# A Hyena-style block with a SwiGLU feed-forward: residuals added from PSUM by VectorE, the half-filled 14th down chunk padded to 128 rows, and a new order of all engines

## The chip, the cores and the metric

The kernel runs on one core of a Trainium2 chip. TensorE multiplies (PE in the profile), VectorE (DVE), ScalarE (ACT) and GpSimd (POOL) work on tiles in SBUF, only TensorE writes results to PSUM, and DMA queues move data; SyncE (SP) issues most DMAs, GpSimd some. Each engine runs its own list of instructions in order and waits on semaphores for the others. The metric is the device time in microseconds of one execution: before the change a median of 253.91 us of 3 runs (253.81 to 254.88).

## What is computed

The input has 2048 tokens of 640 channels. A layer norm of `q` gates a long causal convolution, and a SwiGLU feed-forward follows; both have a residual. `ln` is a layer norm without weights, `*conv*` a causal convolution over the whole sequence.

```
kv  = (causal 4-tap filter of k, per channel) * v
y   = kv *conv* ssm_k  +  kv * ssm_D          # reference: rfft, product, irfft
h   = q + ln(q) * y
out = h + (silu(ln(h) @ w_gate) * (ln(h) @ w_up)) @ w_down      # 640 -> 1728 -> 640
```

1728 hidden columns are 13 chunks of 128 and one chunk of 64.

## The kernel before

The sequence is cut into four blocks of 512 tokens (block 0 to 3). The convolution is done with small Fourier transforms as matrix products with tables of cosines and sines, block against block. The names of the tasks carry the block:

- `tp` the taps as matmuls, `ke` and `kv` their evacuation from PSUM and the product with v;
- `kt`, `kf`, `xf` the transposed filter and the forward transforms, `kte`, `kfe`, `xfe` their evacuations to SBUF, `kb`, `xb` the butterflies on VectorE;
- `p02` and so on the products of spectra (block of x, block of y) on VectorE, L783, `yb` the butterflies before the inverse transform (L561 or, for blocks 2 and 3, L651);
- `iv` the inverse transform on TensorE (L939, L944), followed by evacuation on ScalarE (L954), gate by VectorE (L961), mean and square sums on ScalarE (L860, L862), variance on VectorE (L855), the power -0.5 on GpSimd (L857), normalisation (L1001 or L995) and a transposing DMA by SyncE (`ht`, L450) into `hnT`;
- `fg`, `fu` gate and up products on TensorE (L1049) for 256 tokens at a time, `sg` the silu (L1057), `su`, `sv` the evacuation of up (L1062, L1066, L1068), `mu` their product on VectorE (L1070);
- `dn` the down product of 128 tokens by 640 columns (L1135; the last tile of block 3 in two parts, L1012), `rs` its residual.

**The 14th down chunk.** It has 64 rows of `w_down`, and a matmul of 64 rows occupies half of TensorE's array. With `PAIR = True` the kernel keeps the left 320 columns of that chunk in partitions 0 to 63 and the right 320 in partitions 64 to 127 (`WdC`, `WdD`). A copy `gd` (L1112 on VectorE, L1111 on ScalarE) puts the hidden values of that chunk into partitions 64 to 127 too, and the two matmuls of 64 rows run at the same time. Every other token tile starts with the pair instead of ending with it, so that two pairs can meet.

**The residual.** For the blocks in `RD = (0, 1, 2)` ScalarE or VectorE moves the down product plus the mean of q (q is kept centred) from PSUM to the single buffer `RB` (L1151, L1152), and GpSimd issues a DMA that adds `RB` to `xh` in SBUF (`ra`, L568). SyncE then issues the output DMA (`out`, L1164). For block 3 VectorE does both in one `scalar_tensor_tensor` that reads PSUM (L1156).

**What sets the order.** `PLAN` holds, for each engine, the order of all tasks as numbers, and for each PSUM tile one of four units of two banks. The code adds waits where the data, or the earlier user of a unit, asks for it. Which engine does an evacuation is settled by the list in which it stands. The numbers count the tasks, so removing tasks renumbers the lists.

Of the kernel before, what the change touches and what calls it, by code (L numbers as in the profile page):

```python
# [50 lines left out]
class _Graph:  # L51
# [131 lines left out]
    def emit(self, block):  # L183
# [84 lines left out]
    "act":  # L268
# [9 lines left out]
    "dve":  # L278
# [15 lines left out]
        "806 ",  # L294
    "units":
        "0113201022031012033321231021332312133313321010001232312221313201230311022320230103301222001112012120120312322323013103"
        "23101021312302023330210213103130021301200122003201320321302",
    "fills": {
        "wb0": ["zmem", 3],
        "k0t4.0": ["zmem", 1],  # L300
# [945 lines left out]
```

## Time and profile before

| what | value |
|---|---|
| median of 3 runs | 253.91 us (253.81 to 254.88) |
| the profiled execution's own time | 254.13 us |
| its span, first to last instruction | 252.2 us |
| PE, DVE, ACT, POOL busy | 96%, 78%, 73%, 23% |
| granted TensorE clock | 1.000 |
| the copies `gd` on VectorE and on ScalarE | 5 of 0.22 us, 3 of 0.41 us |
| the residual DMAs `xh<-RB` | 12 of 160 KB, median 2.9 us from issue to landing |

The profile is one execution. Times in it are microseconds from the first instruction. A row such as `L783 DVE TENSOR_TENSOR tt<-XH,C 128x2560 bf16` gives the line of the kernel, the engine, the operation, what it writes and reads, and the shape; `xN` is a count. A number in square brackets is idle time of the engine just before, with what ended it. VectorE's instructions overlap at their ends by some hundredths, so what one costs in a dense stretch is the distance from its start to the next start.

### The profile page before, as it was taken

What the parts mean: (1) busy time and instruction counts of PE and PEld (TensorE: products, weight loads), DVE (VectorE), ACT (ScalarE), POOL (GpSimd) and SP (SyncE); (2) the same over time, 40 slices, a digit from 0 to 9 for tenths busy, and PEclk for the clock granted to TensorE, in tenths of its full rate; (3) what the DMA queues carried; (4) which work ended last, traced back from release to release, by engine and by line L of the source; (5) the groups of instructions that cost most, each with busy time, mean ns of one, the idle gap of its engine ahead of it and who ended that gap; (6) DMA issues with size and microseconds to landing.
All of it is one profiled execution on the core that took longest, in us unless ns stands there. A gap on an engine that the chain in (4) does not pass through costs nothing.

```text
span 252.2 us, 5601 instructions
## 1 busy us (share of the span) xinstructions
PE 243.4 (96%) x2405; PEld 190.7 (76%) x2405; DVE 195.5 (78%) x249; ACT 184.7 (73%) x303; POOL 58.7 (23%) x62
## 2 busy tenths in 40 slices
PE   7998997999999999999999999999999999999995
PEld 3776574688887867888888765888886678888763
DVE  2899999999989999999999896989959321312322
ACT  2499999999897994678999699478982856543500
POOL 1000033443113457602103333211141122100000
PEclk9999999999999999999999999999999999999999
DMA  6999999989994465999914718795871144300003
GB/s 212 338 316 222 389 381 292 142 154 169 274 176 78 141 104 109 174 169 216 208 19 76 189 26 82 169 232 99 146 140 26 23 85 79 81 0 3 0 29 104
DMA packets 39063, 37.04 MB, mean 147 GB/s; under 512 B 21235, under 2 KB 34046, under 8 KB 39038
## 3 DMA queue, kind: packets, MB, share of 16 engines
q1 hardware_dynamic: 31648, 23.56, 35.0%
q0 software_dynamic: 7376, 13.11, 30.7%
q8 instruction: 19, 0.31, 0.5%
q14 instruction: 6, 0.05, 0.0%
q10 hardware_dynamic: 14, 0.01, 0.0%
HBM read 16.29 MB, written 2.62 MB: 75 GB/s over the span
## 4 chain that ended last, share of the span: by engine, by line
PE 73%; DVE 11%; DMA 8%; ACT 5%; issue 1%; SPq 0%; DVEq 0%
PE ps L1049 45%; PE ps L1135 18%; PE ps L581 4%; DMA kvo<-in_A_v_dram 3%; DVE C L561 2%; PE ps L944 2%; DVE tt L783 2%; DMA hnT<-qo 2%; PE ps L1012 2%; DMA k0n<-in_A_k_dram 2%; PE ps L732 1%; DVE kvo L755 1%; DVE Y L783 1%; DMA xh<-RB 1%; DVE kvo L748 1%
## 5 line engine op out<-in xcount | busy, mean ns | idle before, releaser
L1135 PE MATMUL ps<-Wd,gu 128*128 128x320 bf16 (+1 forms) x420 | 58.4, 300 | 0.3 <-ACT qo L954 0.3
L1135 PEld LDWEIGHTS ps<-Wd,gu 128*128 128x128 bf16 (+1 forms) x420 | 38.9, 97 | 18.7 <-issue 2.8
L783 DVE TENSOR_TENSOR tt<-XH,C 128x2560 bf16<-128x2560 bf16 (+1 forms) x29 | 45.1, 1576 | 0.2
L1070 DVE TENSOR_TENSOR gu<-gu,ub 128x1024 bf16<-128x1024 bf16 (+1 forms) x32 | 19.9, 621 | 20.9 <-ACT gu L1057 12.9
L1057 ACT ACTIVATE gu<-ps 128x1024 bf16<-128x1024 f32 (+1 forms) x32 | 29.0, 913 | 8.7 <-PE ps L1049 8.5
L1049 PE MATMUL ps<-hnT,GB 128*128 128x256 bf16 x280 | 34.2, 273 | 0.0
L1049 PE MATMUL ps<-hnT,UB 128*128 128x256 bf16 x280 | 33.7, 273 | 0.0
L1062 ACT ACTIVATE ub<-ps 128x1024 bf16<-128x1024 f32 x24 | 24.5, 1020 | 12.4 <-PE ps L1049 9.7
L1049 PEld LDWEIGHTS ps<-hnT,UB 128*128 128x128 bf16 x280 | 27.4, 98 | 3.3
L1049 PEld LDWEIGHTS ps<-hnT,GB 128*128 128x128 bf16 x280 | 27.2, 98 | 3.3
L1049 PE MATMUL ps<-hnT,UA 128*128 128x256 bf16 x240 | 28.8, 273 | 0.0
L1049 PE MATMUL ps<-hnT,GA 128*128 128x256 bf16 x240 | 28.2, 273 | 0.4 <-DMA hnT<-qo 0.4
L1049 PEld LDWEIGHTS ps<-hnT,GA 128*128 128x128 bf16 x240 | 23.4, 98 | 3.5 <-DVE OS L458 0.8
L1049 PEld LDWEIGHTS ps<-hnT,UA 128*128 128x128 bf16 x240 | 23.3, 98 | 3.1 <-ACT XH L455 0.2
L857 POOL TENSOR_TENSOR mv<-mv,half 128x1 f32<-128x1 f32 x16 | 15.7, 982 | 32.9 <-DVE mv L855 28.5
L581 PE MATMUL ps<-KT,tab 128*128 128x320 bf16 x128 | 19.4, 300 | 2.3 <-DVE KT L457 1.1
L860 ACT ACTIVATE qo<-xh 128x640 bf16<-128x640 bf16 x28 | 20.6, 736 | 1.2 <-DMA hnT<-qo 0.5
L954 ACT ACTIVATE qo<-ps,one,st 128x640 bf16<-128x640 f32 x16 | 13.8, 883 | 8.1 <-PE ps L939 7.1
L568 POOL DMA_DIRECT2D xh<-RB x12 | 10.8, 899 | 38.0 <-ACT RB L1151 31.6
L581 PEld LDWEIGHTS ps<-KT,tab 128*128 128x128 bf16 x128 | 11.3, 98 | 8.8 <-DVE KT L457 1.4
L857 POOL TENSOR_TENSOR st<-st,half 128x4 f32<-128x4 f32 x4 | 7.2, 1792 | 38.7 <-DVE st L852 31.4
L862 ACT ACTIVATE qo<-xh,mv 128x640 bf16<-128x640 bf16 x16 | 13.2, 830 | 0.2
(115 smaller groups left out, 377.0 us busy)
## 6 DMA issues: line engine op xcount, KB each, us to landing
C<-US POOLq DMA_DIRECT2D x6, 640.0 KB, 6.6
kc<-in_A_ssm_k_dram SPq DMA_DIRECT2D x4, 640.0 KB, 9.9
xh<-in_A_q_dram SPq DMA_DIRECT2D x4, 640.0 KB, 6.9
out_dram<-xh SPq DMA_DIRECT2D x15, 160.0 KB, 1.9
kvo<-in_A_v_dram SPq DMA_DIRECT2D x3, 640.0 KB, 7.6
xh<-RB POOLq DMA_DIRECT2D x12, 160.0 KB, 2.9
C<-C POOLq DMA_DIRECT2D x2, 640.0 KB, 7.6
Wd<-in_B_w_down_dram SPq DMA_DIRECT2D x1, 1280.0 KB, 11.8
```

The costliest lines, as they stand in the source:

```text
L568: return g.add(name, "pool", lambda e, n: e.dma_start(dst, src, accum_op=ALU.add, max_dma_last_dim=4096), ("acc", 2 * int(np.prod(dst.shap ...
L581: last = e.matmul(pt.f(c, W), tab[:, f, cs, j], src[:, j, c * W:(c + 1) * W], start=(j == js[0]), stop=(j == js[1]))
L783: g.add(nm, "dve", lambda e, n_: e.tensor_tensor(out=d, in0=a, in1=b, op=op), ("sb", n * D), r=[a, b], w=[d])
L857: g.add(name + "r", "pool", lambda e, n: e.tensor_tensor(out=dst, in0=tmp, in1=hf, op=ALU.pow), ("pp", 4), r=[tmp, half[:]], w=[dst])
L860: g.add(name + "m", "act", lambda e, n: e.activation(out=junk, in_=x, func=ACTF.Identity, scale=-1.0 / D, accum_out=sm), ("aa", D, 0), r=[ ...
L862: g.add(name + "s", "act", lambda e, n: e.activation(out=junk, in_=x, func=ACTF.Square, bias=sm, accum_out=sq), ("aa", D, 1), r=[x, sm], w ...
L954: g.add(nm + "e", "act", lambda e, n, pt=pt, q2=q2, s=s, j=j: e.activation(out=q2, in_=pt.f2(W), func=ACTF.Identity, scale=s[:, 3, j:j + 1 ...
L1049: last = e.matmul(pt.f(q // 2, 256, o=256 * (q % 2)), w[:, c, f0:f0 + P], hnT[:, c, cols], start=(c == 0), stop=(c == NC5 - 1))
L1057: g.add("sg%d.%d%d" % (i, h, gp), "act", lambda e, n, pa=pa, gv=gv, nf=nf: e.activation(out=gv, in_=pa.f(0, 256 * nf).rearrange("p (f x) - ...
L1062: g.add("su%d.%d%d" % (i, h, gp), "act", lambda e, n, pb=pb: e.activation(out=ub[:].rearrange("p b x -> p (b x)"), in_=pb.f(0, 1024), func ...
L1070: g.add("mu%d.%d%d" % (i, h, gp), "dve", lambda e, n, gv=gv, ubv=ubv: e.tensor_tensor(out=gv, in0=gv, in1=ubv, op=ALU.mult), ("sb", 256 * ...
L1135: last = e.matmul(pt.f(c, W), gu[k, fb, col(i, j)], Wd[k, fb, c * W:(c + 1) * W], start=st, stop=sp)
```

## The change

Three settings change, and with them the whole plan.

1. `RD = (0,)`: in blocks 1 and 2 VectorE adds the residual from PSUM by `scalar_tensor_tensor`, as in block 3. Eight evacuations to `RB` (five on ScalarE, three on VectorE) and eight adding DMAs of GpSimd are gone; eight instructions on VectorE are new.
2. `PAIR = False`: the 14th chunk of `w_down` lies whole in partitions 0 to 63, a new memset `wz` clears that chunk's 128 rows first, and the down product uses 128 rows for it. The eight copies `gd`, the load `WdD`, and the order with the pair first are gone. The product of gate and up for chunks 12 and 13 becomes two instructions, `mu` of 128 partitions and `mv` of 64 (so that rows 64 to 127 keep the gate's other half, which meets zero rows of `Wd`).
3. The plan's numbers are new for all engines and for the PSUM units. In it GpSimd's powers (L857) stand at other places against VectorE's instructions that read PSUM.

```diff
@@ PLAN: "pe", "act", "dve", "pool", "sp", "units": all numbers are new
-    "pe":
-        "19 21 25 28 24 27 30 33 31 34 23 26 29 32 64 67 61 40 38 69 73 75 43 71 47 57 49 51 45 53 55 79 81 77 83 142 91 89 306 "
...
+    "pe":
+        "20 22 26 24 25 28 31 34 29 27 32 35 30 33 65 62 68 41 39 70 74 72 48 76 50 56 54 46 52 78 58 44 84 82 80 90 143 92 94 "
...
-    RD = (0,1,2)
+    RD = (0,)
...
-    PAIR = True
+    PAIR = False
...
         kload(3)
+        if not PAIR:
+            g.add("wz", "pool dve", lambda e, n: e.memset(Wd[:, 13, :], 0.0), ("pm", D), w=[Wd[:, 13, :]])
...
-                        k = slice(0, P) if fb < 13 else slice(FL * c, FL * c + FL)
+                        k = slice(0, P) if fb < 13 or not PAIR else slice(FL * c, FL * c + FL)
...
+                    if nf == 2 and not PAIR:
+                        for nm, a, b in (("mu", gu[:, 12, cols], u12), ("mv", gu[0:FL, 13, cols], u13)):
+                            g.add("%s%d.%d%d" % (nm, i, h, gp), "dve", lambda e, n, a=a, b=b: e.tensor_tensor(out=a, in0=a, in1=b, op=ALU.mult),
+                                  ("sb", 256), r=[a, b], w=[a])
+                        continue
...
-                if col(i, j).start // P % 2:
+                if PAIR and col(i, j).start // P % 2:
                     seq = [13] + seq[:-1]
...
-                                k = slice(0, P) if fb < 13 else slice(FL * c, FL * c + FL)
+                                k = slice(0, P) if fb < 13 or not PAIR else slice(FL * c, FL * c + FL)
```

How the new numbers move instructions is shown at three places.

VectorE, while the first inverse tiles of block 0 are gated (`KT` and `KO` are the transposed filter and the odd half of its transform, `C` the spectra of the filter blocks, `xh<-xh,qo` the gate). Before:

```order
L561 TENSOR_TENSOR Y_53<-Y_53 128x2560
L457 COPY KT_67<-ps 128x2x640
L961 TENSOR_TENSOR xh_88<-xh_88,qo_103 128x640
L748 TENSOR_TENSOR kvo<-XT_59,kvo 128x16x4x32
L561 TENSOR_TENSOR C_51<-C_51,KO_81 128x2560
L961 TENSOR_TENSOR xh_88<-xh_88,qo_101 128x640
L855 TENSOR_SCALAR mv_109<-mv_109 128x1
L561 TENSOR_TENSOR C_51<-C_51,KO_81 128x2560
L457 COPY KT_68<-ps 128x2x640
```

Now (the lines after the new memset are shifted by two, so L457 and L458 are L455 and L456):

```order
L561 TENSOR_TENSOR Y_53<-Y_53 128x2560
L961 TENSOR_TENSOR xh_88<-xh_88,qo_103 128x640
L748 TENSOR_TENSOR kvo<-XT_59,kvo 128x2x4x64
L561 TENSOR_TENSOR C_51<-C_51,KO_81 128x2560
L961 TENSOR_TENSOR xh_88<-xh_88,qo_101 128x640
L455 COPY KT_68<-ps 128x2x640
L855 TENSOR_SCALAR mv_109<-mv_109 128x1
L456 TENSOR_SCALAR KO_82<-ps 128x640
L748 TENSOR_TENSOR kvo<-XT_59,kvo 128x16x4x32
L855 TENSOR_SCALAR mv_107<-mv_107 128x1
L456 TENSOR_SCALAR KO_82<-ps 128x640
```

Two evacuations of the filter's transform (`KO_82<-ps`) have come to VectorE from ScalarE, each behind an instruction that hands GpSimd a power (L855), and the copy `KT_67<-ps` has gone to ScalarE.

VectorE again, before the inverse transform of block 2 (`Y_55` is that block's spectrum; what reads it is `iv2`). Before:

```order
L783 TENSOR_TENSOR Y_55<-Y_55,tt 128x2x1280
L1070 TENSOR_TENSOR gu<-gu,ub 128x4x256
L783 TENSOR_TENSOR tt<-XH_56,C_49 128x2560
L651 TENSOR_TENSOR OS<-Y_55 128x1280
...
L651 TENSOR_TENSOR Y_55<-OS,Y_55 128x2x1280
L885 TENSOR_SCALAR st_0_105<-st_0_105 128x4
L1070 TENSOR_TENSOR gu<-gu,ub 128x2x256
L1112 COPY gu<-gu 64x256
L748 TENSOR_TENSOR kvo<-XT_59,kvo 128x16x4x32
```

Now:

```order
L783 TENSOR_TENSOR Y_55<-Y_55,tt 128x2x1280
L855 TENSOR_SCALAR st_0_105<-st_0_105 128x4
L783 TENSOR_TENSOR tt<-XH_56,C_49 128x2560
L1161 SCALAR_TENSOR_TENSOR xh_89<-ps,st_1_106,xh_89 128x640
L783 TENSOR_TENSOR tt<-XH_56,C_49 128x2560
...
L651 TENSOR_TENSOR Y_55<-OS,Y_55 128x2x1280
L1072 TENSOR_TENSOR gu<-gu,ub 128x256
L1072 TENSOR_TENSOR gu<-gu,ub 64x256
L651 TENSOR_TENSOR Y_55<-OS,Y_55 128x2x1280
```

The first residual of block 1 (L1161, reading PSUM) now stands in VectorE's list ahead of the last butterflies of block 2, and the products `kvo` (which wait for the load of block 3's v) stand behind the second of the last two `Y_55<-OS,Y_55`.

TensorE, from the second down tile of block 1 (`dn1.1`) to the first gate or up product of block 2 (the first row that reads `hnT`; L619 is `xf3`). Before:

```order
L1135 MATMUL ps<-Wd,gu 128x320 x28
L939 MATMUL ps<-Y_55,itab 128x320 x8
L1135 MATMUL ps<-Wd,gu 128x320 x28
L939 MATMUL ps<-Y_55,itab 128x320 x4
L619 MATMUL ps<-kvo,tab 128x320 x2
L939 MATMUL ps<-Y_55,itab 128x320 x4
L619 MATMUL ps<-kvo,tab 128x320 x2
L1135 MATMUL ps<-Wd,gu 128x320 x28
L619 MATMUL ps<-kvo,tab 128x320 x12
L1049 MATMUL ps<-hnT,GA 128x256 x30
```

Now:

```order
L1140 MATMUL ps<-Wd,gu 128x320 x28
L939 MATMUL ps<-Y_55,itab 128x320 x8
L1140 MATMUL ps<-Wd,gu 128x320 x28
L619 MATMUL ps<-kvo,tab 128x320 x2
L939 MATMUL ps<-Y_55,itab 128x320 x4
L619 MATMUL ps<-kvo,tab 128x320 x4
L939 MATMUL ps<-Y_55,itab 128x320 x4
L619 MATMUL ps<-kvo,tab 128x320 x4
L1140 MATMUL ps<-Wd,gu 128x320 x28
L619 MATMUL ps<-kvo,tab 128x320 x4
L1049 MATMUL ps<-hnT,UA 128x256 x20
L619 MATMUL ps<-kvo,tab 128x320 x2
```

The same work lies between the first inverse tiles of block 2 and its first feed-forward product, but for two matmuls of `xf3` that now come after that product. Up to `dn0.0b`, to `iv2.0` and to `dn2.0` TensorE's lists hold the same tasks before and now, in other orders.

More of the change, by code (lines that the diff above doesn't have):

```diff
@@ L260 @@
     "pe":
[7 rows of a table removed]
[L268 removed]
[9 rows of a table removed]
[L278 removed]
[9 rows of a table removed]
[7 rows of a table added]
+    "act":
[8 rows of a table added]
+    "dve":
[9 rows of a table added]
     "pool":
[L289 to L290 removed]
+        "19 17 15 16 14 129 178 169 130 162 202 187 196 228 201 230 229 340 285 360 361 398 370 380 371 289 381 293 403 297 390 "
+        "391 408 417 521 522 419 420 555 546 564 573 672 580 585 693 698 686 720 711 729 688 738 ",
     "sp":
[L292 to L294 removed]
+        "0 2 3 8 4 6 9 7 235 10 12 13 300 11 231 301 299 233 234 232 239 238 236 477 180 171 237 189 198 286 478 363 373 290 "
+        "383 294 298 476 393 642 466 643 557 548 475 472 469 566 641 575 722 713 640 731 634 740 786 789 795 637 631 792 798 ",
     "units":
[L296 to L297 removed]
+        "0131203110220301021321303213011023033223020032211131102001123210123102210322012012233100012011303303302221012002031022"
+        "12213113232113023112031302031203212013002033132022301203321",
     "fills": {
@@ L1138, in ffn @@
                     fbs = [f for f in part if f != "id"]
-                    mode = (int(part[0] == 13), int(part[-1] == 13))
+                    mode = (int(part[0] == 13), int(part[-1] == 13)) if PAIR else ()
                     g.add("dn%d.%d%s" % (i, pos(i, j), "b" if len(parts) > 1 and part is parts[1] else ""), "pe", mm,
-                          ("mm", W, 2 * len(part) - (13 in part)) + mode,
+                          ("mm", W, 2 * len(part) - (PAIR and 13 in part)) + mode,
                           r=[gu[:, f, col(i, j)] for f in fbs] + [Wd[:, f] for f in fbs] + ([x, ident] if "id" in part else []),
```

6 lines of the change are left out of this document (1 added, 5 removed), and 47 rows, old and new, of the table PLAN.

## The prediction

> **What bounds the kernel now.** I read the page first, then busy times by stretch, then waits and the chain inside the one stretch that is not full.
>
> ```profile
> span 252.2 us, 5601 instructions
> PE 243.4 (96%) x2405; PEld 190.7 (76%) x2405; DVE 195.5 (78%) x249; ACT 184.7 (73%) x303; POOL 58.7 (23%) x62
> PE 73%; DVE 11%; DMA 8%; ACT 5%; issue 1%; SPq 0%; DVEq 0%
> ```
>
> TensorE is busy nearly throughout, but 78% of VectorE is an average over two very unlike parts:
>
> ```profile
> 42.50:78.70 36.20, 36.19 (x307) 29.32 (x308) 35.30 (x38) 34.15 (x60) 11.31 (x10) 1.00 0.96 182
> 78.70:144.15 65.45, 65.45 (x772) 53.04 (x771) 64.93 (x70) 53.24 (x87) 23.54 (x20) 1.00 0.72 137
> 144.15:157.50 13.35, 12.57 (x91) 7.94 (x88) 10.04 (x20) 12.56 (x25) 4.61 (x6) 1.00 0.49 52
> 157.50:249.50 92.00, 92.00 (x780) 74.72 (x780) 48.18 (x70) 50.46 (x81) 14.33 (x16) 1.00 0.39 82
> ```
> ```profile
> 8.50:143.67 135.17, 131.59 (x1477) 103.77 (x1474) 133.52 (x157) 118.68 (x194) 38.84 (x32) 1.00 0.87 197
> ```
>
> The columns are busy times of PE, PEld, DVE, ACT, POOL. Until 144.15, where block 2's first inverse tile (`iv2.1`) starts, TensorE and VectorE are both full: VectorE idles 135.17 - 133.52 = 1.65 us from 8.50 to 143.67, the moment it has finished `yb2.4`, the spectrum that `iv2.1` reads. Behind 157.50 TensorE alone is full and VectorE half idle. Between lies the only hole of TensorE after 42.50, 0.78 us. So an instruction more on VectorE costs time if it stands ahead of `yb2.4`, and nothing behind 157.50; one less on TensorE counts everywhere unless VectorE is later.
>
> The hole comes from this chain (start, length, what):
>
> ```profile
> 137.53 7.55 DMA kvo<-in_A_v_dram
> 145.08 0.02 issue
> 145.10 1.23 DVE kvo L748
> 146.33 0.41 DVE xh L961
> 146.74 0.02 issue
> 146.76 0.84 ACT qo L860 x2
> 147.60 0.02 issue
> 147.63 0.92 ACT qo L862 x2
> ...
> 150.35 1.55 ACT qo L954 x2
> ...
> 152.81 4.60 DMA hnT<-qo
> 157.41 0.09 issue
> 157.50 2.56 PE ps L1049 x22
> ```
>
> Block 3's v, loaded late, holds VectorE's list at 145.10; gates, moments and a 4.60 us transpose follow, and TensorE starts block 2's feed-forward only at 157.50.
>
> **The 14th chunk, on TensorE.** Four rows of the timeline of PE (start, length):
>
> ```profile
> 140.37 3.95 PE L1135 MATMUL ps<-Wd,gu 64*128 64x320 bf16 x28
> 144.15 1.25 PE L939 MATMUL ps<-Y,itab 128*128 128x320 bf16 x8
> 145.24 3.94 PE L1135 MATMUL ps<-Wd,gu 128*128 128x320 bf16 x28
> 149.11 0.72 PE L939 MATMUL ps<-Y,itab 128*128 128x320 bf16 x4
> ```
>
> Eight full matmuls take 145.24 - 144.15 = 1.09, 0.136 each, so a tile of 28 full ones takes 3.81. The tile that ends with a pair takes 149.11 - 145.24 = 3.87: the concurrent pair saves 0.136 and the two changes between half and full rows cost 0.20. So a lone pair is worth -0.06 when removed; two pairs that meet share the changes and are worth +0.07; a pair beside the taps, which change the array anyway, +0.14. In the order before I count seven lone ones, two couples, three beside taps, and the split last tile, where 64 rows gain nothing and the changes cost 0.28. The taps of blocks 2 and 3 now stand together, two changes of 0.20 fewer. Sum over the kernel: -0.42 + 0.14 + 0.41 - 0.28 - 0.40, about -0.55 us; what lies behind 157.50 (two lone, two couples, the split tile) is -0.12 + 0.14 - 0.28, about -0.3.
>
> The Trainium skill, page "TensorEngine Tiling (Array Packing)", section "Theoretical Speedup", says the opposite of this edit: a contraction of at most 64 rows gains up to 2x by tiling. By that alone, 15 tiles would grow by 0.136 each, +2.0 us. The row above sides with the same page's "Key Properties", that a change of mode drains the engine.
>
> **What VectorE has to do before `yb2.4`.** Prices from these rows:
>
> ```profile
> 36.10 0.82 DVE L457 COPY KT<-ps 128x1280 bf16<-128x1280 bf16 x1
> 36.84 0.48 DVE L961 TENSOR_TENSOR xh<-xh,qo 128x640 bf16<-128x640 bf16 x1
> ```
> ```profile
> L1156 DVE SCALAR_TENSOR_TENSOR xh<-ps,st,xh 128x640 bf16<-128x640 f32 x3 | 2.7, 884 | 6.4 <-PE ps L1135 6.4
> L1070 DVE TENSOR_TENSOR gu<-gu,ub 128x512 bf16<-128x512 bf16 x8 | 3.4, 419 | 1.0 <-ACT ub L1068 0.9
> L871 DVE TENSOR_SCALAR xh<-xh,mvs 128x640 bf16<-128x640 bf16 x4 | 1.5, 375 | 0.0
> L1112 DVE COPY gu<-gu 64x256 bf16<-64x256 bf16 x5 | 1.1, 221 | 0.2
> ```
>
> An evacuation of 0.82 costs 0.74 from start to next start, so I take 0.07 off each duration.
>
> - Evacuations that move from ScalarE: `xf0.110`, `kf2.110`, `kf2.011`, `kf3.010`, 4 x 0.74, and the taps' `ke2.4` of 512 columns, 0.60. To ScalarE go `kf0.011` and `kte2.1`, -1.43.
> - The first residual of block 1, L1161: 0.88 - 0.07 = 0.81. The other seven lie behind `yb2.4`, where VectorE has room.
> - The centring `la1.3x` comes from ScalarE, 0.30.
> - Three products of 512 columns (0.42) become two of 256. No row has that form; the bounds are half of 0.42 and the 0.22 of the copy of 64x256, so 0.02 each more. Two copies `gd` go, -0.44, and one small copy goes to GpSimd, -0.10.
>
> Sum: 2.96 + 0.60 - 1.43 + 0.81 + 0.30 + 0.06 - 0.54, about +2.8 us. The idle 1.65 does not all stay:
>
> ```profile
> DVE gu L1070 <- ACT gu L1057: 0.7, 1, 0.7
> DVE C L561 <- ACT C L455: 0.2, 1, 0.2
> ```
>
> The 0.7 was a wait for `sg0.02`, which now stands ahead of two other silus and a square sum in ScalarE's list. So `yb2.4` ends at 143.67 + 2.8 - 0.7, about 145.7 (144.8 with no idle left, 146.4 with all of it), and `iv2.1` starts 1.6 us later than at 144.15. TensorE has the same tasks up to there and cannot use the time: it waits first for the `kvo` products of block 2, which VectorE ends near 110 as before, while TensorE's list now comes to `xf2` one product of 20 matmuls earlier; the rest it waits at `iv2.1`. This term is +1.6, between +0.6 and +2.3.
>
> **From `iv2.1` to block 2's feed-forward.** TensorE's list holds 86 matmuls of 320 columns there, 11.70 us at 0.136, where 13.35 passed. The residual DMAs are gone and `out1.0` no longer waits for one, so v arrives in time; the gates stay behind `yb2.5`. A new wait appears: `dn1.3` takes the PSUM unit of an `xf3` tile, and ScalarE reaches that tile's evacuation only after two moves of the inverse (1.55 together), two mean sums and two square sums (0.84 and 0.92 each), and three more evacuations of about 0.72; starting 0.7 after `iv2.1` and waiting once for VectorE's gate, it ends near 8.0, while TensorE is there after 54 matmuls, 7.35. That is 0.65, so 12.35, and two `xf3` matmuls (0.27) are still owed: -0.73. The transposes end in time: the last normalised tile is ready about 7.7 after `iv2.1`, and even 4.60 more is 12.3. Bounds: -1.4 without the new wait, 0 if the hole only changes its cause.
>
> **What lies beside other work.** The memset of the 14th chunk (GpSimd, first microseconds), one load for two, five evacuations and three copies less on ScalarE behind 78.70, the seven later residuals, and eight adding DMAs less (GpSimd's issue of 0.90 each) save nothing by themselves: outside the hole no wait of TensorE ends on them. If that cover were gone, seven residuals would cost 5.7 us.
>
> GpSimd's powers:
>
> ```profile
> L857 POOL TENSOR_TENSOR mv<-mv,half 128x1 f32<-128x1 f32 x16 | 15.7, 982 | 32.9 <-DVE mv L855 28.5 <-DVE st L891 4.5
> ```
> ```profile
> 154.41 0.55 POOL L857 TENSOR_TENSOR mv<-mv,half 128x1 f32<-128x1 f32 x1 [2.37 <-DVE mv L855]
> ```
>
> They take 0.98 on average and 0.55 at best, so 16 could shrink by 6.9 us together, nearly all off the path: I count 0. (The Trainium skill, "SBUF — State Buffer", "Who interferes with whom", has VectorE instructions with two SBUF inputs shut GpSimd's reads out; the row's spread agrees with it.)
>
> **Sum.** +1.6 - 0.7 - 0.3 = +0.6 us. The profiled execution's own time is 254.13, 1.9 above its span and 0.2 above the median of 253.91: 254.7 by it, 254.5 as a median.
>
> **Rivals.**
>
> *The room is found again* (faster). VectorE loses all idle time, `yb2.4` ends at 144.8, the PSUM wait does not appear: +0.6 - 1.4 - 0.5 = -1.3, 252.6. For it: 1.65 us of idle is there to lose. Against: most of that is spread over 157 instructions.
>
> *VectorE's late work holds PSUM* (slower). All idle stays and the hole is filled by waits for evacuations: +2.3 + 0 - 0.3 = +2.0, 255.9. For it: the first down tile of block 1 keeps its unit until VectorE comes to L1161, after six more products.
>
> *A weight load shuts out the transposes* (slower, the clearest on that side). SyncE's list now issues `WdA` ahead of block 0's transposes `ht0.2` and `ht0.3`; before it came after them.
>
> ```profile
> Wd<-in_B_w_down_dram SPq DMA_DIRECT2D x1, 1280.0 KB, 11.8
> Wd<-in_B_w_down_dram SPq DMA_DIRECT2D x1, 800.0 KB, 4.9
> hnT<-qo SPq DMA_TRANSPOSE x16, 3.2
> ```
> ```profile
> 66.63 1.25 PE L1049 MATMUL ps<-hnT,GA 128*128 128x256 bf16 x10
> ```
>
> `WdA` waits for the last `kf3` (near 56 us in TensorE's new order); with 11.8 and 3.2 behind it the tokens land at 71.3, and TensorE wants them near 66.6. 4.7 us late, of which the 1.6 us that TensorE is ahead of VectorE are free: +3.1 on top, 257.6. It decides from a landing later than 68.2. Against: part of the 11.8 was queueing behind the transposes, and 800 KB took 4.9.
>
> *Full rows cost two microseconds.* If the pairs did halve the chunk, nine tiles behind `iv2.0` would grow by 0.136 instead of shrinking: +1.6 on the forecast, 256.1. The row of 3.87 against 3.81 speaks against it. (This is the mechanism of the rule of the Trainium skill's page "TensorEngine Tiling (Array Packing)" named above.)
>
> **How the numbers follow.** Forecast 0.50, room found 0.15, PSUM held 0.15, load in the way 0.15, full rows 0.05. The predicted time is 254.5; alone that case spans 253.4 to 255.6. For 8 in 10 the range takes in the first rival and the second, not all of the third: 252.6 to 257.0. Half a per cent, 1.27 us, is what a measurement here tells from no change: faster means under 252.64, slower over 255.18. Faster: half of the first rival and a little of the forecast, 0.10. Slower: the last three rivals and a quarter of the forecast's spread, less what falls short, 0.36. Within: 0.54.
>
> **What would show it.** VectorE's stretch from 8.5 to the end of `yb2.4` longer by 1.3 to 2.7 us with over 135.5 us busy; the first L939 of block 2 near 145.7; TensorE idle shortly before it and near 110; the hole before block 2's feed-forward shorter than 0.78 with the release no longer a DMA; a down tile of 28 matmuls in 3.81. Wrong would be: VectorE done with `yb2.4` by 144.2, or idle of TensorE near 66 on `hnT`.

## The result, and the profile after

The changed kernel takes 260.65 us (median of 6 runs, 260.06 to 261.23) against 254.33 for the kernel before on the same chip: 1.0247 times as long, with a 95% interval of 1.0218 to 1.0276. Forecast were 254.5, between 252.6 and 257.0. The forecast was wrong, and the range too. In this document a time is the median of all runs of a kernel, while the ratios leave out two runs that were slower throughout, one of `gap_many` (259.94) and one of `gap_three` (260.06).

The page of the profiled execution (its own time is 260.99): the span, the busy times, and the shares of the chain that ended last.

```profile
span 258.6 us, 5585 instructions
PE 244.5 (95%) x2405; PEld 193.6 (75%) x2405; DVE 198.5 (77%) x257; ACT 178.7 (69%) x293; POOL 58.7 (23%) x57
PE 52%; DVE 31%; POOL 6%; ACT 4%; DMA 4%; issue 1%; SPq 0%; ACTq 0%
```

GpSimd (POOL) had no share worth printing in the chain before; now it has 6%, and VectorE 31% where it had 11%. Busy times by stretch of the changed kernel, cut at the same events as the rows in the prediction (end of `yb2.4`; `iv2.1` to block 2's first feed-forward product; the rest). The columns are PE, PEld, DVE, ACT, POOL.

```profile
8.50:150.41 141.91, 133.28 (x1491) 104.83 (x1488) 135.49 (x161) 116.41 (x189) 43.83 (x33) 1.00 0.79 182
150.90:163.94 13.04, 12.01 (x88) 8.02 (x86) 11.77 (x21) 12.26 (x25) 2.79 (x5) 1.00 0.63 77
163.94:258.60 94.66, 91.98 (x782) 76.42 (x782) 48.01 (x72) 47.07 (x76) 10.13 (x12) 1.00 0.34 72
```

The first stretch is 141.91 - 135.17 = 6.74 us longer. VectorE's work in it grew by 135.49 - 133.52 = 1.97, its idle time from 1.65 to 141.91 - 135.49 = 6.42. The second stretch is 0.31 shorter (13.04 against 13.35), the third 0.04 shorter (94.66 against 252.2 - 157.50 = 94.70). So the loss lies wholly ahead of `yb2.4`, and 4.77 of the 6.74 are added idle time of VectorE. VectorE's waits between 77 and 151 us:

```profile
DVE tt L783 <- DMA Y<-tt: 3.4, 1, 3.4
DVE xh L961 <- ACT qo L954: 1.9, 1, 1.9
```

Both begin on GpSimd. The timeline of the changed kernel around the first (start, length):

```profile
77.36 0.15 DVE L855 TENSOR_SCALAR st<-st 128x4 f32<-128x4 f32 x1
77.43 1.48 DVE L561 TENSOR_TENSOR OS<-Y 128x2560 bf16<-128x2560 bf16 x1
77.60 5.30 POOL L857 TENSOR_TENSOR st<-st,half 128x4 f32<-128x4 f32 x1 [4.40 <-DVE st L855]
78.83 0.37 DVE L881 TENSOR_SCALAR xh<-xh,st 128x640 bf16<-128x640 bf16 x1
...
79.12 1.48 DVE L561 TENSOR_TENSOR Y<-Y 128x2560 bf16<-128x2560 bf16 x1
...
80.53 1.48 DVE L783 TENSOR_TENSOR tt<-XH,C 128x2560 bf16<-128x2560 bf16 x1
...
83.00 1.66 ACT L954 ACTIVATE qo<-ps,one,st 128x640 bf16<-128x640 f32 x2 [2.12 <-POOL st L857]
83.92 0.49 DVE L961 TENSOR_TENSOR xh<-xh,qo 128x640 bf16<-128x640 bf16 x1 [1.91 <-ACT qo L954]
```

`la1r` raises four values in each partition to a power, and took 5.30 us. VectorE meanwhile ran four instructions, each starting before the one ahead had ended, and GpSimd ended 0.9 us after the last of them (82.90 against 82.01). ScalarE's move L954 needs the result, VectorE's gate L961 needs that move. In the kernel before, the same power:

```profile
76.03 0.42 DVE L1070 TENSOR_TENSOR gu<-gu,ub 128x512 bf16<-128x512 bf16 x1
76.21 1.13 POOL L857 TENSOR_TENSOR st<-st,half 128x4 f32<-128x4 f32 x1 [2.55 <-DVE st L855]
...
76.48 0.22 DVE L1112 COPY gu<-gu 64x256 bf16<-64x256 bf16 x1
76.73 1.49 DVE L561 TENSOR_TENSOR OS<-Y 128x2560 bf16<-128x2560 bf16 x1
```

There `gd0.0`, one of the copies that the change removes, waits for the multiply ahead of it (76.03 + 0.42 = 76.45, start 76.48) and the next instruction waits for the copy (76.70, start 76.73): VectorE is empty twice for 0.03 us, and the power gets through. The second wait, in the chain of the changed kernel:

```profile
88.30 6.29 POOL mv L857
94.65 0.29 POOL mv L993
94.94 6.45 DMA Y<-tt
101.40 0.02 issue
101.42 1.50 DVE tt L783
```

The power `iv1.0r`, of one value per partition, lasted 6.29 us; behind it in GpSimd's list stood the transfer `p02.e`, so it was issued at 94.94 where the kernel before had it at 88.56, and VectorE stood 3.4 us before `p12.0a`. Over the kernel:

```profile
L857 POOL TENSOR_TENSOR mv<-mv,half 128x1 f32<-128x1 f32 x16 | 19.8, 1239 | 57.9 <-DVE mv L855 53.4 <-DVE st L893 4.5
L857 POOL TENSOR_TENSOR st<-st,half 128x4 f32<-128x4 f32 x4 | 11.2, 2789 | 40.6 <-DVE st L852 23.5 <-DVE st L855 17.1
```

### The profile page after: what moved, and what is told of

It is laid out like the page before. It is cut to its first block, busy times and chain, and to the rows that moved or that the text cites. A ratio compares the mean times of both kernels' runs of the same rounds, so it can differ in the third digit from the quotient of the medians.

```text
span 258.6 us, 5585 instructions
## 1 busy us (share of the span) xinstructions
PE 244.5 (95%) x2405; PEld 193.6 (75%) x2405; DVE 198.5 (77%) x257; ACT 178.7 (69%) x293; POOL 58.7 (23%) x57
## 4 chain that ended last, share of the span: by engine, by line
PE 52%; DVE 31%; POOL 6%; ACT 4%; DMA 4%; issue 1%; SPq 0%; ACTq 0%
PE ps L1049 32%; PE ps L1140 13%; DVE tt L783 9%; DVE Y L783 5%; POOL mv L857 3%; DVE C L561 3%; DMA Y<-tt 2%; PE ps L581 2%; POOL st L857 2%; DVE C L783 2%; DVE XH L561 2%; ACT qo L954 2%; DMA k0n<-in_A_k_dram 2%; PE ps L1012 1%; PE ps L732 1%
## 5 line engine op out<-in xcount | busy, mean ns | idle before, releaser
L1140 PE MATMUL ps<-Wd,gu 128*128 128x320 bf16 x420 | 59.5, 299 | 0.0
L1140 PEld LDWEIGHTS ps<-Wd,gu 128*128 128x128 bf16 x420 | 41.0, 98 | 15.7 <-ACT XH L453 0.2
L857 POOL TENSOR_TENSOR mv<-mv,half 128x1 f32<-128x1 f32 x16 | 19.8, 1239 | 57.9 <-DVE mv L855 53.4
L1075 DVE TENSOR_TENSOR gu<-gu,ub 128x1024 bf16<-128x1024 bf16 x24 | 16.4, 685 | 15.5 <-ACT gu L1057 10.5
L581 PE MATMUL ps<-KT,tab 128*128 128x320 bf16 x128 | 20.4, 300 | 1.3 <-ACT KT L453 0.9
L857 POOL TENSOR_TENSOR st<-st,half 128x4 f32<-128x4 f32 x4 | 11.2, 2789 | 40.6 <-DVE st L852 23.5
L954 ACT ACTIVATE qo<-ps,one,st 128x640 bf16<-128x640 f32 x16 | 13.8, 883 | 8.9 <-PE ps L939 6.7
L1161 DVE SCALAR_TENSOR_TENSOR xh<-ps,st,xh 128x640 bf16<-128x640 f32 x11 | 9.7, 878 | 7.8 <-PE ps L1140 7.8
L862 ACT ACTIVATE qo<-xh,mv 128x640 bf16<-128x640 bf16 x16 | 13.2, 830 | 0.1
```

The costliest lines, as they stand in the source:

```text
L581: last = e.matmul(pt.f(c, W), tab[:, f, cs, j], src[:, j, c * W:(c + 1) * W], start=(j == js[0]), stop=(j == js[1]))
L857: g.add(name + "r", "pool", lambda e, n: e.tensor_tensor(out=dst, in0=tmp, in1=hf, op=ALU.pow), ("pp", 4), r=[tmp, half[:]], w=[dst])
L862: g.add(name + "s", "act", lambda e, n: e.activation(out=junk, in_=x, func=ACTF.Square, bias=sm, accum_out=sq), ("aa", D, 1), r=[x, sm], w ...
L954: g.add(nm + "e", "act", lambda e, n, pt=pt, q2=q2, s=s, j=j: e.activation(out=q2, in_=pt.f2(W), func=ACTF.Identity, scale=s[:, 3, j:j + 1 ...
L1075: g.add("mu%d.%d%d" % (i, h, gp), "dve", lambda e, n, gv=gv, ubv=ubv: e.tensor_tensor(out=gv, in0=gv, in1=ubv, op=ALU.mult), ("sb", 256 * ...
L1140: last = e.matmul(pt.f(c, W), gu[k, fb, col(i, j)], Wd[k, fb, c * W:(c + 1) * W], start=st, stop=sp)
```

## The experiments

**Theory A:** GpSimd's short arithmetic starves while VectorE runs its two-input instructions without a pause; the new order does that at two powers that others wait for. **Theory B:** the two edits cost the time by their work, and the long powers are a by-product. **Theory C:** GpSimd or its transfers are late by themselves. Of the tasks named here, `la1r` and `iv1.0r` are powers, `iv1.0b` is the multiplication behind the second, all on GpSimd; `p02.e` is a transfer that GpSimd issues. Each kernel has one profiled execution. All ratios below are to the kernel before on the same chip, with the 95% interval.

| kernel | us | ratio | `la1r` us | what it is |
|---|---|---|---|---|
| gap_one | 261.33 | 1.0271 [1.0239, 1.0303] | 2.21 | changed kernel, copy behind `yb1.0` |
| gap_two | 258.78 | 1.0178 [1.0154, 1.0202] | 5.30 | copy behind `p02.c` |
| gap_both | 257.81 | 1.0127 [1.0095, 1.0160] | 2.21 | both |
| gap_many | 257.03 | 1.0088 [1.0055, 1.0120] | 2.21 | ten copies |
| gap_three | 258.54 | 1.0135 [1.0089, 1.0181] | 5.37 | three copies |
| empty_three | 257.04 | 1.0107 [1.0085, 1.0129] | 2.21 | three real gaps |
| before_train | 254.46 | 1.0013 [0.9998, 1.0028] | 2.20 | kernel before, two instructions moved |
| before_new_seg | 260.91 | 1.0252 [1.0223, 1.0281] | 2.20 | kernel before, new VectorE order in block 1 |
| change_old_order | 257.44 | 1.0127 [1.0086, 1.0169] | 6.01 | both edits, old order |
| change_old_gap | 257.33 | 1.0136 [1.0102, 1.0170] | 6.08 | the same with copies |
| add_only | 256.38 | 1.0095 [1.0065, 1.0125] | 1.13 | residual adds, old order |
| pair_only | 256.50 | 1.0074 [1.0051, 1.0096] | 6.01 | 128-row chunk, old order |
| pair_gap | 256.47 | 1.0109 [1.0069, 1.0150] | 6.08 | copy at `gd0.0`'s place |
| pair_late_gap | 256.02 | 1.0070 [1.0046, 1.0093] | 6.08 | copy behind `yb1.0` |
| pair_copy | 255.02 | 1.0013 [0.9993, 1.0034] | 1.20 | `gd0.0`, `gd0.1` kept |
| hybrid | 255.50 | 1.0052 [1.0030, 1.0074] | 6.08 | both edits, old order up to `iv2.1` |
| hybrid_late_gap | 256.16 | 1.0088 [1.0060, 1.0116] | 6.08 | the same, copy behind `yb1.0` |
| hybrid_copy | 253.95 | 0.9976 [0.9961, 0.9990] | 1.20 | the same, `gd0.0`, `gd0.1` kept |

### Openings in the changed kernel

The edits are shown shortened, here and below.

```diff
+ g.add("gate0", "dve", tensor_scalar(out=warm[:, 0:4], in0=half[:, 0:4], scalar1=1.0, op0=mult))
  VectorE: ... yb1.0 [+gate: one, both] la1.3x ... p02.c [+gate: two, both] iv1.2g ...
```

> The changed kernel with one instruction more and nothing moved: behind yb1.0 VectorE runs a copy of 4 f32 values, one input, that nothing reads. Theory A (GpSimd's power starves while VectorE runs tensor_tensor after tensor_tensor; it starts when an instruction with one small input comes, as la1r waited from 77.60 to 82.4 behind yb1.0, la1.3x, yb1.1 and p02.d): la1r (L857, 128x4) takes under 2.3 us in place of 5.30, iv1.0e starts near 80.3 in place of 83.00, VectorE's 1.91 us and TensorE's 1.71 us of idle time near 83 go, and the time falls by 1.0 to 1.9, to 258.8-259.7; iv1.0r still takes about 6. Theory B (the seven residual adds and the 12 extra multiplies on VectorE make it late, and the long powers are a by-product): the time stays at 260.65 within 0.4. Theory C (the power is long for a reason of GpSimd's own, such as its transfers): la1r stays over 4 us, the time unchanged.

> The changed kernel with the same copy of 4 values behind p02.c alone, 1.5 us after iv1.0r is released. Theory A: iv1.0r (128x1) takes about 1.5-2.0 us in place of 6.28, the transfer p02.e behind it on GpSimd is issued near 90.8 in place of 94.94 and lands by 97.5, VectorE's 3.40 us wait before p12.0a goes, and the time falls by 2.5 to 3.8, to 256.9-258.2; la1r still takes over 5. Theory B: unchanged within 0.4. Theory C (p02.e itself is slow, or its queue): iv1.0r is short but VectorE still waits over 2 us for p02.e, and the time falls by under 1.

> Both copies in the changed kernel. Theory A: the two gains add, since VectorE's two waits (1.91 and 3.40 us) stand one after the other: 254.7 to 256.2, within 0.5 of what was forecast for the change (254.5) at best, and within 2% of the kernel before. yb2.4 ends near 145.5 in place of 150.41. Theory B: 260.2 to 261.1. Theory C: in between, over 257.5.

(The expectation of gap_one counts seven residual adds and 12 multiplies more; the traces show eight of each.) GpSimd's rows in gap_both:

```profile
77.68 2.21 POOL L857 TENSOR_TENSOR st<-st,half 128x4 f32<-128x4 f32 x1 [4.33 <-DVE st L855]
...
86.46 1.89 POOL L857 TENSOR_TENSOR mv<-mv,half 128x1 f32<-128x1 f32 x1 [5.20 <-DVE st L893]
88.42 4.81 POOL L993 TENSOR_TENSOR mv<-mv 128x1 f32<-128x1 f32 x1
93.18 1.31 POOL L568 DMA_DIRECT2D Y<-tt  x1
```

Both powers are short, and the time falls by 2.84, where B expected no change. But A's number (254.7 to 256.2) is missed: the starving passed to the next instruction, a plain multiplication, 4.81 us, and `p02.e` is still late, so VectorE still waits 3.4 us. In gap_two that multiplication took 4.01, and the time fell by 1.87 where 2.5 to 3.8 were expected. In gap_one (261.33, expected 258.8 to 259.7) the freed `la1r` gained nothing: `iv1.0r` then took longer than ever,

```profile
85.94 7.08 POOL L857 TENSOR_TENSOR mv<-mv,half 128x1 f32<-128x1 f32 x1 [5.20 <-DVE st L893]
```

past eight instructions of VectorE, one of them a `tensor_scalar` of one value with one input.

```diff
  gap_many: one such copy behind each of yb1.0 p02.d p02.c p02.b p12.0b mu0.12 p12.1b iv1.3g p12.1c p03.a
  gap_three: behind yb1.0, p02.c, p02.b
  empty_three: at the same three places two copies, the second reading the first
+ t.deps.add(by[a])     # the first waits for the end of the instruction ahead of it
```

> The changed kernel with ten of the 4-value copies on VectorE between yb1.0 and p03.a (behind yb1.0, p02.d, p02.c, p02.b, p12.0b, mu0.12, p12.1b, iv1.3g, p12.1c, p03.a), nothing moved. With two of them the time was 257.81, and a wait of the same kind had only moved on to the next GpSimd instruction: iv1.0b, one multiplication of 128x1, took 4.81 us, and p02.e behind it in GpSimd's list was issued at 93.18 and landed after VectorE had waited 3.41 us for it. Theory A (any arithmetic of GpSimd starves in VectorE's train, not the power alone): with ten gaps no GpSimd instruction between 77 and 100 takes over 2.4 us, p02.e is issued near 90.0, the 3.4 us go, and the time is 254.2 to 255.6 (ten gaps cost some 0.7 us of VectorE in it). Theory B (what is left over the kernel before is the price of the residual adds and the 128-row chunk): 257.3 to 258.6.

> The changed kernel with three copies of 4 values: behind yb1.0 and p02.c as in gap_both (257.81), and a third behind p02.b for iv1.0b, which had taken 4.81 us there and held up the transfer p02.e. Theory A: iv1.0b under 2 us, p02.e issued near 90, VectorE's 3.41 us before p12.0a gone, 254.9 to 256.2. If the time stays over 257, what is left over the kernel before is not this chain.

> The changed kernel, nothing moved, with a real gap of VectorE at the three places of gap_three (behind yb1.0, p02.c and p02.b): two 4-value copies each, the first waiting for the end of the instruction ahead of it, the second for the end of the first, so that VectorE runs empty for some 0.2 us, where the single copies ran overlapped with their neighbours. The single copy behind yb1.0 had let la1r in in three kernels (2.21 us) and not in three others (5.37 to 6.08), and gap_three spread from 255.95 to 258.81. Theory A, second form (GpSimd gets in for certain where VectorE is empty, and by chance where a one-input instruction passes overlapped): la1r 2.0-2.4, iv1.0r 1.7-2.1, iv1.0b under 2, p02.e issued near 90, both of VectorE's waits (1.91 and 3.40) gone, 255.2 to 256.8. Theory A, first form (one input is enough): no better than gap_three's 258.54, la1r long again. Theory B: over 257.5 with short powers.

gap_many issues `p02.e` at 90.31 and the 3.4 us are gone, but its time (257.03, expected 254.2 to 255.6) is missed, and a multiplication at 94.02 still took 4.23. gap_three rids `p02.e` of its delay too (issued at 91.85), but its `la1r` was shut out again, 5.37 us past the very copy behind `yb1.0` that had let it in in the three other kernels, and 258.54 misses the expected 254.9 to 256.2; three of its four runs spread from 255.95 to 258.81. empty_three, where VectorE really runs empty, holds both (`la1r` 2.21, `iv1.0r` 1.87, `iv1.0b` 0.35, `p02.e` at 90.48), within 256.71 and 258.10. So at least 3.6 us of the changed kernel's 6.3 are the starving, with some 0.8 us of added copies still in the 257.04 (VectorE is busy for 136.30 up to `yb2.4`, against 135.49). The expected 255.2 to 256.8 is just missed: a wait that the long transfer wait had hidden took 1.7 us.

```profile
DVE mv L855 <- ACT qo L862: 1.7, 1, 1.7
```

The chain that ended last in empty_three leads from this wait back to GpSimd:

```profile
94.39 4.13 POOL mv L993
98.52 0.83 POOL xh L568
99.35 1.54 POOL mv L993
...
100.92 0.56 ACT qo L995
...
101.74 0.77 ACT RB L1156
102.52 0.82 ACT qo L862 x2
...
103.36 0.15 DVE mv L855
```

VectorE's variance `iv1.3v` (L855) stands behind a square sum (L862) that ScalarE's list has after a residual (L1156) and a normalisation (L995), and the normalisation waited 1.44 us for a multiplication on GpSimd. That one took 1.78 us. The one ahead of it took 4.16 beside six overlapping instructions of VectorE and ended 0.06 after VectorE ran empty: the starving again, at the next GpSimd instructions, where no opening had been made. What is left over the kernel before is 2.6 us by the profiled spans (254.8 against 252.2). Up to `yb2.4` VectorE works 2.78 us more (0.81 of it the copies) and idles 1.19 more; the stretch from `iv2.1` to block 2's first product is 1.32 shorter (12.03).

### The kernel before with the new order

```diff
- la1v mu0.03 gd0.0 yb1.0 ...  iv1.0v p02.c iv1.1v p02.b
+ mu0.03 gd0.0 la1v yb1.0 ...  iv1.0v iv1.1v p02.c p02.b      # before_train
+ mu0.03 gd0.0 la1v yb1.0 la1.3x yb1.1 p02.d ... p12.1c       # before_new_seg: the changed kernel's list
```

> The kernel before with two small instructions of VectorE moved and none added: la1v (it releases the power la1r) behind mu0.03 and gd0.0 in place of ahead of them, and iv1.1v ahead of p02.c in place of behind it. So la1r meets yb1.0, p02.d, mu0.10 and yb1.1 in a row, and iv1.0r meets p02.c, p02.b, iv1.2g, mu0.11, p12.0b, mu0.12, p12.0d and so on until the copy gd0.1. VectorE's work is the same to the instruction, and there are no added residual adds. Theory A: la1r takes about 5 us in place of 1.13 and iv1.0r 5 to 7.5 in place of 1.80; the time rises by 2.5 to 5.5, to 256.8-259.8. Theories B and C: it stays within 0.5 of the kernel before.

> The kernel before, with its own edits untouched, but VectorE's list from la1v to p12.1c in the changed kernel's order, la1.3x on VectorE among it (it was on ScalarE), gd0.0 ahead and gd0.1 behind mu0.13. No other engine's list is changed. The first try in this direction (two instructions moved) left the time as it was, since la1r came in after 2.20 us and iv1.0r after 0.56. Theory A: with the whole train la1r takes 3 to 5.5 us or iv1.0r / iv1.0b 3 to 7, VectorE idles over 2 us before iv1.0g or p12.0a, and the time is 256.5 to 260.5. Theory B: 253.8 to 254.8.

Neither shows A. In before_train `la1r` got in after `yb1.0`, between two overlapping two-input instructions, and `iv1.0r` at once (0.56): nothing lost, the expectation missed. In before_new_seg `la1r` met the four instructions of VectorE past which it took 5.30 in the changed kernel, and took 2.20. The time came out as A expected (and 0.4 above its upper end), but for another reason: no power was long ahead of 100 us, and VectorE waited for ScalarE, whose list had stayed the old one (the granted clock was 0.993 over the span, 0.91 from 100 to 115 us, where TensorE stood still for 2.9; what that adds is not separated):

```profile
DVE gu L1070 <- ACT gu L1057: 2.4, 2, 1.9
DVE mv L855 <- ACT qo L862: 1.7, 1, 1.7
DVE kvo L748 <- ACT XT L455: 1.6, 1, 1.6
```

It shows how much a list changed on one engine alone can cost. For the starving it shows only that such a train does not always cause it.

### Each edit alone, in the old order

```diff
- RD = (0,1,2)
+ RD = (0,)            # add_only;  pair_only: PAIR = False;  change_old_order: both
```

> The residual adds of blocks 1 and 2 alone on the order of the kernel before, the paired chunk and its copies gd kept: rs1.0, rs1.1, rs1.3, rs2.0 and rs2.2 from ScalarE to VectorE as one add out of PSUM each, the nine transfers ra1 and ra2 gone from GpSimd. Theory A: la1r stays at 1.1 and no power takes over 2.4; VectorE has one add (rs1.0, 0.88) more ahead of yb2.4 and the 0.8 us hole of TensorE takes part of it: 253.9 to 255.3. Theory B (these adds are the cause): 257 or more.

> The 128-row chunk alone on the order of the kernel before: one load less, no copies gd, split multiplies, all 28 matmuls of a down tile on 128 rows; the residual adds as before. Forecast of the document: the lone pairs removed give back 0.55 us over the kernel, VectorE loses its two copies and gains the split. Theory A: 253.2 to 254.6, up to 256 if la1r, whose opening at 76.5 was the copy gd0.0, now waits for yb1.0, p02.d, mu0.10 and yb1.1. Theory B with this edit as the cause: 256 to 260.

> The whole change (residual adds of blocks 1 and 2 on VectorE, 14th chunk on 128 rows, multiplies split) in the order of the kernel before: the old lists of every engine, with the new instructions put in at the nearest place (each residual add where ScalarE read that tile, each split multiply behind its sibling), so without the new lists. Theory A (the new order is the cause, the two edits cost next to nothing): 253.6 to 255.4, that is within 0.5% of the kernel before, though the copies gd0.0 and gd0.1 that broke VectorE's train are gone and la1r may wait up to 4 us more. Theory B (the edits are the cause, by VectorE's extra work): 258 to 261.

change_old_order (257.44, `la1r` 6.01) falls in neither theory's range: with both edits and the old order half of the loss, 3.2 us, is still there, so the new order alone is not the cause. Its `la1r` starves there too, since the copies `gd0.0` and `gd0.1` are gone. add_only costs 2.25 us with a short `la1r`: a price of the edit in that order, which A had put at 1.2 at most and B at 2.9 at least. (Eight transfers go in it, not nine: 12 `xh<-RB` before, four left.)

```profile
8.50:144.70 136.20, 132.60 (x1486) 104.39 (x1480) 134.30 (x157) 118.28 (x193) 37.93 (x31) 1.00 0.85 194
144.84:158.73 13.89, 12.87 (x89) 7.90 (x89) 11.51 (x23) 11.41 (x23) 1.89 (x3) 1.00 0.23 25
158.73:254.20 95.47, 92.39 (x780) 74.64 (x780) 50.51 (x73) 48.92 (x79) 10.74 (x12) 1.00 0.33 71
```

Against the kernel before: +1.03 up to `yb2.4` (0.78 of it work, the one residual forecast at 0.81), +0.54 between, +0.77 behind. pair_only costs 2.3 us, half a microsecond over A's upper end and within B's range, and has the starving in the open:

```profile
76.90 0.48 DVE L1073 TENSOR_TENSOR gu<-gu,ub 128x256 bf16<-128x256 bf16 x2
77.08 6.01 POOL L858 TENSOR_TENSOR st<-st,half 128x4 f32<-128x4 f32 x1 [2.54 <-DVE st L856]
77.31 1.48 DVE L562 TENSOR_TENSOR OS<-Y 128x2560 bf16<-128x2560 bf16 x1
```

VectorE's next instruction starts (77.31) before the split multiplies end (77.38); the copy that stood between is gone. Whether this is the whole of the 2.3 was asked of four kernels:

```diff
  pair_gap:       mu0.03 mv0.03 +gate0 yb1.0 p02.d ... mu0.13 mv0.13 +gate1
  pair_late_gap:  mu0.03 mv0.03 yb1.0 +gate0 p02.d
  pair_copy:      mu0.03 mv0.03 +gd0.0 yb1.0 p02.d ... mu0.13 mv0.13 +gd0.1
  change_old_gap: as pair_gap, with both edits
```

> The 128-row chunk alone on the order of the kernel before, as in pair_only (256.50, where la1r took 6.01 us and VectorE stood 1.92 + 0.28 us before iv1.0g and iv1.1g), with two of the 4-value copies on VectorE just where the copies gd0.0 and gd0.1 had stood (behind mv0.03 and mv0.13). Theory A (the whole 2.3 us of pair_only are the opening that the copy gd0.0 had given): la1r takes under 1.5 us, the two stalls go, and the time is 253.4 to 254.4. Theory B (the split multiplies or the 128 rows cost): 256 to 256.8.

> The whole change in the old order, as in change_old_order (257.44, with la1r at 6.01 us), with the two copies of 4 values where gd0.0 and gd0.1 stood. Theory A: la1r under 1.5 us, VectorE's 2.2 us before iv1.0g and iv1.1g go, and with the price of the added adds the time is 254.0 to 255.5. Theory B: within 0.5 of 257.4.

> The 128-row chunk alone in the old order, as pair_only, with one copy of 4 values, but behind yb1.0, 1.4 us later than in pair_gap. There the copy had stood at 77.00, 0.22 us after GpSimd began la1r (76.78), and did not let it in: la1r took 6.08 and the time was 256.47, so the expectation of theory A fell. Theory A in its second form (a power asks for its inputs some tenths of a microsecond after it begins; only an opening behind that counts): as behind yb1.0 in the changed kernel, where the copy opened in all three runs, la1r takes 2.0-2.4, VectorE's 1.91 and 0.28 us go, 253.6 to 254.6. Theory B in its second form (la1r's length is a by-product, the split multiplies or the 128 rows set the 2.3 us): 256.0 to 257.

> The 128-row chunk alone in the old order, as pair_only, but the two copies gd0.0 and gd0.1 of the kernel before are kept, each in its old place (they write rows 64 to 127 of the 14th chunk, which now meet zero rows of the weights). gd0.0 waits for the end of mv0.03 and so leaves VectorE empty for some hundredths of a microsecond on both sides, where the 4-value copy of pair_gap ran overlapped with its neighbours. Theory A, second form: with that gap la1r comes in as in the kernel before, 1.0 to 1.5 us, and the time is 253.6 to 254.6; if only the lateness of the opening counts and not the gap, la1r stays near 6 and the time at 256 to 257. Theory B: 256 to 257 with a short la1r.

The copy of 4 values did nothing in three kernels (pair_gap, pair_late_gap and change_old_gap, 6.08 us each), early or late; the expectations fell, and with them the idea that one input is enough or that only the moment counts. The old copy, which does no useful work here, brings `la1r` to 1.20:

```profile
77.14 0.48 DVE L1073 TENSOR_TENSOR gu<-gu,ub 128x256 bf16<-128x256 bf16 x2
77.32 1.20 POOL L858 TENSOR_TENSOR st<-st,half 128x4 f32<-128x4 f32 x1 [2.10 <-DVE st L856]
...
77.65 0.22 DVE L1118 COPY gu<-gu 64x256 bf16<-64x256 bf16 x1
77.90 1.49 DVE L562 TENSOR_TENSOR OS<-Y 128x2560 bf16<-128x2560 bf16 x1
```

It starts 0.03 after the multiplies end, and `yb1.0` 0.03 after it. VectorE's wait of 1.9 us before `iv1.0g` is gone, and the time is 255.02, not to be told from the kernel before (ratio 1.0013, interval 0.9993 to 1.0034; pair_only 1.0074, 1.0051 to 1.0096). The tasks of GpSimd are those of pair_only, and the two copies were added on VectorE, which speaks against theory C. The median misses the expected 253.6 to 254.6, and the 0.55 us that the missing pairs should give back do not show in it.

### Both edits, each stretch in its better order

```diff
  every engine: the old list up to iv2.1, the changed kernel's list behind it
+ elif i in RD or (i, j) == (1, 0):     # block 1's first residual as before
  hybrid: gate0, gate1 at gd's places;  hybrid_late_gap: gate0 behind yb1.0;  hybrid_copy: gd0.0, gd0.1 kept
```

> Both edits, with the old order of every engine up to the matmul iv2.1 of block 2 (the paired chunk's copies replaced by the two 4-value copies, the first residual of block 1 still by ScalarE and a transfer) and the changed kernel's order behind it, which ran from iv2.1 to block 2's first feed-forward matmul in 12.1-13.0 us against 13.35 in the kernel before. Theory A: the head as in the kernel before (yb2.4 near 143.7 to 144.2, no power over 2.4 us), and behind it 0.5 to 1.2 us less: 252.6 to 253.9, the first version under the kernel before. Theory B: over 255.

> The hybrid order (old order up to iv2.1, the changed kernel's behind it; 255.50, with la1r at 6.08 us and VectorE's 1.91 + 0.28 us before iv1.0g and iv1.1g still in it), with the one copy of 4 values moved behind yb1.0. Theory A, second form: these 2.2 us go, yb2.4 ends near 144.2, and the time is 252.8 to 254.0, at or under the kernel before. Theory B: 255 to 256.

> The hybrid order with both edits (255.50 with a 4-value copy that opened nothing), with the old copies gd0.0 and gd0.1 kept in their old places as in pair_copy (255.02, where la1r took 1.20). Theory A, second form: la1r near 1.2, VectorE's 2.2 us before iv1.0g and iv1.1g gone, 253.2 to 254.8, that is the kernel before within 0.5%: the two edits are worth nothing much either way once the order is free of the starving. Theory B: 255.3 or more.

The first two miss for the reason just shown (6.08 us). With the old copies:

```profile
8.50:144.91 136.41, 132.23 (x1490) 105.11 (x1485) 133.64 (x158) 118.92 (x194) 39.24 (x32) 1.00 0.86 196
145.30:157.39 12.09, 12.01 (x89) 8.02 (x87) 11.45 (x20) 11.31 (x24) 1.56 (x3) 1.00 0.32 29
157.39:252.00 94.61, 91.98 (x782) 76.39 (x782) 48.44 (x74) 48.01 (x77) 10.69 (x13) 1.00 0.36 72
```

253.95 us, 0.24% under the kernel before (0.10 to 0.39%): the only version under both kernels, by very little. The new order with its residual adds is worth 13.35 - 12.09 = 1.26 between `iv2.1` and block 2's feed-forward, and the adds cost nothing behind it (94.61 against 94.70); VectorE's stretch up to `yb2.4` is 1.24 longer than before, mostly idle time (2.77 against 1.65).

## Why the prediction was wrong

- **What bounds the kernel: right.** VectorE up to `yb2.4` sets the time, TensorE behind it; `iv2.1` starts 6.75 us later and the end moves by 6.4.
- **VectorE's work: right in kind, too high.** +2.8 forecast, +1.97 measured.
- **"The idle 1.65 does not all stay": wrong sign.** Forecast were 0.7 us less idle time, measured 4.77 more. It took the waits that were there and looked which would go; it did not ask what the new neighbours of each short instruction would do.
- **The step that failed: "16 could shrink by 6.9 us together, nearly all off the path: I count 0."** The powers were priced on one side only. The row's spread (0.55 at best, 0.98 on average) already showed that they can take longer. The rule of the Trainium skill ("SBUF — State Buffer", "Who interferes with whom") that was named beside it gives a reason: a VectorE instruction with two SBUF inputs contends with GpSimd's reads. The new order, in which the copy `gd0.0` was gone and `la1v` stood right ahead of `yb1.0`, `la1.3x`, `yb1.1` and `p02.d`, could have been held against that spread. What the runs showed in its place: two powers of 5.30 and 6.29 us on the path, VectorE's waits of 1.9 and 3.4 us behind them, and at least 3.6 us back when VectorE was made to pause. The term should have had an upper bound of what VectorE has queued, 5 us and more at each power, with ScalarE's evacuation (1.9) and GpSimd's next transfer (3.4) behind it. No rival had it.
- **From `iv2.1` to block 2: mechanism half right.** 12.35 forecast for the stretch, 13.04 measured, against 13.35 before. The load of v no longer holds anything; the PSUM wait at `dn1.3` did not appear; TensorE waited at block 2's first product instead, by the profile for a variance on VectorE (L855):

```profile
163.94 1.25 PE L1049 MATMUL ps<-hnT,UA 128*128 128x256 bf16 x10 [1.03 <-DVE mv L855]
```

  Where block 1 is not late (empty_three 12.03, hybrid_copy 12.09) the stretch is even shorter than forecast.
- **The 14th chunk: tile right, sum over the kernel not seen.** A down tile of 28 full matmuls takes 206.72 - 202.92 = 3.80, less than the tile with a lone pair (3.87); full rows cost nothing, and that rival falls. Behind 163.94 forecast were -0.3, with two matmuls (0.27) owed; measured is -0.04, which agrees. The -0.55 over the whole kernel does not show in pair_copy. Of the two sections named in the prediction from the Trainium skill's page "TensorEngine Tiling (Array Packing)", the rows side with "Key Properties" (a change of mode drains the engine) against a gain by "Theoretical Speedup".

```profile
202.92 3.97 PE L1140 MATMUL ps<-Wd,gu 128*128 128x320 bf16 x28
206.72 0.71 PE L939 MATMUL ps<-C,itab 128*128 128x320 bf16 x4
```

- **The residual adds: cost 0 held only in the new order** (94.61 behind block 2's start in hybrid_copy, 95.47 in add_only, 94.70 before). The cover named in the prediction is there in the changed kernel's list, and not where the adds are put in at the nearest place of the old one.
- **The load in the way: refuted.** `WdA` took 7.6 us, not 11.8, and TensorE does not idle near 66. (The sum there, 56 + 11.8 + 3.2, is 71.0 and not 71.3.)
- **Room found again, and PSUM held by late work: neither.** (The first of these adds up with the whole kernel's -0.5 for the chunk where the forecast counts only the -0.3 behind 157.50.) TensorE's idle near 110 us came as forecast, and not from the starving alone: from 100 to 125 us it is 3.3 us in five waits, 0.51 of them for `kvo`, and in empty_three still 1.8 in four, the 0.51 among them.

What stays open: why `la1r` got in between overlapping instructions in some kernels (before_train and before_new_seg; behind the 4-value copy in gap_one, gap_both and gap_many) and not in others (pair_gap, pair_late_gap, gap_three and the changed kernel). What held for every power in all twenty kernels is that it ended within 0.92 us of the first moment, begun behind its own start, in which VectorE was empty, if only for 0.03 us: each `la1r` of over 5 us ended 0.90 us after such a moment began, the longest `iv1.0r` (gap_one) 0.43. Of the multiplications one (1.78 us, in three kernels) let such a moment pass that came 0.22 after its start. Open too is how the rest of the 6.3 us divides: the starving that empty_three leaves and the price of the edits in VectorE's stretch were not measured apart.

## What to carry to other kernels

Before an order is changed, look at each short GpSimd instruction that someone waits for, and read what VectorE does in the next five microseconds: a train of two-input instructions can make it last as long as the train. A copy that looks superfluous may be the pause that lets GpSimd in; taking it away cost 1.5 us here, for a length of 0.22. Price an instruction that shares something with another engine by both ends of its spread, not by its mean in the old order.

## What the runs showed of the hardware

The starving was not one instruction long. A power of one value per partition that takes 0.55 us when free took up to 7.08, past eight instructions of VectorE of up to 1.47 each. The same section of the Trainium skill ("SBUF — State Buffer", "Who interferes with whom") says that the loser blocks for the whole instruction that holds the ports; if the next claim were then served in turn, the power would have waited 1.5 us at most, an estimate from the longest of the eight. It is not only the power: one multiplication of 128x1 took 4.81. A transfer's issue on GpSimd was not touched (1.30 to 1.32 us beside such a train, as in the kernel before), which agrees with the remark in that section of the Trainium skill, marked there as inferred, that a tensor_tensor takes only the read side. And an instruction with one input that overlaps its neighbours let GpSimd in in some kernels and not in others.
